# A long convolution with a mixture of experts: four inputs laid in DRAM in the order of their loads

## The chip, the cores and the metric

The kernel runs on one core of a Trainium2 chip. The metric is device microseconds from the start to the end of one execution; less is better. A core has a matrix engine (PE, with its weight loads PEld), VectorE (DVE), ScalarE (ACT), GpSimd (POOL) and SyncE (SP), each with its own stream of instructions, and 16 DMA engines that they share. A DMA is issued by an engine's instruction onto that engine's queue: q1 is SP's, q10 is ACT's, q0 is POOL's. Operands lie in SBUF, in 128 rows (partitions); PE writes to PSUM.

## The reference, cut to what matters

```python
def _attn_ref(x, v, pos_emb, w1, w2):          # x, v: 4 x 11456 x 128, f32
    h_filt = (np.maximum(pos_emb @ w1, 0.0) @ w2) * np.exp(-0.01 * pos)[:, None]
    u = x * v
    L = 2 * S
    Uf = np.fft.rfft(u, n=L, axis=1)
    Hf = np.fft.rfft(h_filt, n=L, axis=0)
    y = np.fft.irfft(Uf * Hf[None, :, :], n=L, axis=1)[:, :S, :]
    return x * y
def _moe_ref(x, w_skip, w_gate, w1, w2):       # 45824 tokens, 8 experts of width 1024
    xc = x[x @ w_skip > 0]
    ...
    y[mask] = gate_w[mask, None] * (np.maximum(xc[mask] @ w1[e], 0.0) @ w2[e])
    out[do_compute] = xc + y
```

The product u of x and v is convolved with a filter that is itself computed from pos_emb, multiplied by x once more, and the tokens with a positive skip score then go through the expert that their gate chooses. This change concerns the convolution and the last multiplication by x.

## The kernel before, in words

The sequence is cut into 3 blocks (NB) of L = 60 x 64 tokens (K1 x N2). A block's transform is done in two stages: matrices over the 60, then, for each of the 60 frequencies, a 128 x 128 matrix over the 64 (with the twiddle factors in it). The 128 channels are split into two halves of 64 (DH), so each stage is passed twice.

**First stage** (class First, L104; `first_phase`, L279). A step handles 8 of the 64 columns of one block and one half of the channels; there are 24 steps to a half (STEPS) and 48 in all. `load` (L143) fetches x and v for a step, 480 KB each, into tiles of 120 rows x 1024 numbers; its DMAs at L150 are on SP's queue. There are three tiles of each (XV), and `ahead` issues a step's load once the tile of three steps before has been multiplied. `mult` (L163) forms u on DVE; in the first pass ACT and DVE split it into a rounded and a remaining part (L169, L170); PE multiplies (L158), ACT copies the sums out of PSUM (L159), and ACT issues one store of 960 KB to x1d in DRAM (L193), in pieces of 1 KB. The filter's own work (`filt`, L197) is dealt out between: its input post, 3 MB in rows of 8 KB on 64 partitions, comes in six loads on ACT's queue (L225); its stores to x1d, 360 KB each in pieces of 768 bytes, are issued by ACT too (L246). The first pass and one step of the second (25 steps) run in this stage.

**Second stage** (`freq_phase`, L306). It goes over 60 pairs of frequencies, 30 to a half. `load` (L332) fetches for each pair its two matrices, c2 (L339, 128 KB), and its data, x1 (L341, 960 KB, rows of 3840 bytes), on SP's queue, three pairs ahead. PE transforms (L372), DVE multiplies by the filter (L366), POOL adds (L368), PE transforms back (L399), ACT copies out (L400), and SP stores to zd (L404). The remaining 23 steps of the first stage's second pass are dealt out among the first 30 pairs.

**Output stage** (`out_phase`, L801). 32 chunks of 3 blocks. `load` (L839) fetches, five blocks ahead, z from zd (L848, 480 KB, pieces of 1 KB) and x once more, ox (L850, 256 KB, 128 rows of 2 KB), on SP's queue. PE does the last transform (L862), DVE multiplies by x (L863), the tokens' scores are taken, and POOL scatters each row to its expert's place in DRAM (L950, 384 indirect DMAs). `START` sets at which step each chunk begins; the first scatter comes in the step of the seventh product. 31 slots of experts' work are dealt out into this stage, and 62 more follow it (`late_slots`).

The host function `arrays` lays out the inputs before the launch, outside the measured time. Before the change `tokens` gives x and v the order (column of 64, row of 60, block, half, batch, channel). One step's load takes from it, for each of its 120 rows, four pieces of 1 KB; rows lie 6 KB apart. c2 lies as (frequency, row, column), and a pair's load takes two pieces of 512 bytes for each row. xo holds a chunk's three blocks side by side, so a block's rows are 2 KB with 6 KB from one to the next.

Of the kernel before, what the change touches and what calls it, by code (L numbers as in the profile page):

```python
# [19 lines left out]
B, S, D = 4, 11456, 128  # L20
E, F = 8, 1024
NB = 3
K1, N2 = 60, 64
L = K1 * N2
H2 = N2 // 2
NS = NB * B
N = L * NS
DH = D // 2
# [23 lines left out]
def tables():  # L52

    k1 = np.arange(K1)
    k2 = np.arange(N2)
    n2 = np.arange(N2)
    n1 = np.arange(K1)
    th = 2 * np.pi * n1[:, None] * (k1[None, :] + 0.25) / K1
    c1 = np.zeros((2, K1, 2, K1, 2))
    c1f = np.zeros((64, 2, 2, K1, 2))  # L60
    for p in range(2):
        c1[p, :, p] = c1f[:K1, p, p] = np.stack([np.cos(th), -np.sin(th)], axis=-1)
    ph = 2 * np.pi * n2[None, :, None] * (k1[:, None, None] + 0.25 + K1 * k2[None, None, :]) / L
    c2 = np.zeros((K1, 128, 128))
    c2[:, :64, :64] = np.cos(ph)
    c2[:, 64:, :64] = np.sin(ph)
    c2[:, :64, 64:] = -np.sin(ph)
    c2[:, 64:, 64:] = np.cos(ph)
    ps = 2 * np.pi * k2[:, None] * n2[None, :] / N2
    c3 = np.zeros((128, 2, 128))  # L70
    c3[:64, 0, :64] = np.cos(ps)
    c3[64:, 0, :64] = -np.sin(ps)
    c3[:64, 0, 64:] = np.sin(ps)
    c3[64:, 0, 64:] = np.cos(ps)
    c3[:64, 1, :64] = -np.sin(ps)
    c3[64:, 1, :64] = -np.cos(ps)
    c3[:64, 1, 64:] = np.cos(ps)
    c3[64:, 1, 64:] = -np.sin(ps)
    c3 = np.ascontiguousarray(c3.reshape(128, 2, 2, 64).transpose(0, 1, 3, 2)).reshape(128, 2, 128)
    al = 2 * np.pi * (k1[:, None, None] + 0.25) * (N2 * n1[None, None, :] + n2[None, :, None]) / L  # L80
    c4 = np.zeros((2 * K1, N2, 64))
    c4[:K1, :, :K1] = np.cos(al) / L
    c4[K1:, :, :K1] = -np.sin(al) / L
    pos = np.arange(S, dtype=np.float32)
    win = np.zeros(NB * L, np.float32)
    win[:S] = np.exp(np.float32(-0.01) * pos)
    winp = np.zeros((2, 64, NB, H2), np.float32)
    winp[:, :60] = win.reshape(NB, 60, 2, H2).transpose(2, 1, 0, 3)
    row = np.arange(128)[:, None] * NS + np.arange(NS)

    e = np.arange(E)
    shift = np.zeros((E, 2, E))
    shift[e, 0, e] = -1
    shift[e[1:], 0, e[:-1]] = 1
    shift[-1, 0, -1] = 0
    shift[:, 1] = e[:, None] <= e[None, :]
    bump = np.where(e < E - 1, CAP, 2 * DUMMY)
    f = np.float32
    winp = winp.transpose(1, 0, 2, 3)
    return {  # L100
        "c1": c1.reshape(2 * K1, 2, 2 * K1).astype(f), "c1f": c1f.reshape(128, 2, 2 * K1).astype(f),
        "c2": c2.astype(f), "c3": c3.astype(f),
        "c4": np.ascontiguousarray(c4.reshape(2 * K1, 2, H2, 64).transpose(0, 2, 1, 3)).astype(f),
        "win": winp.reshape(128, NB * H2), "idb": row.astype(f),  # L104
        "rev": np.tile(np.arange(E, 0, -1, dtype=f), (128, 1)),
        "tri": (np.arange(128)[:, None] < np.arange(128)[None, :]).astype(np.float16),
        "iota": np.tile(np.arange(NTAB, dtype=f), (E, 1)),
        "shift": shift.astype(f), "bump": bump.reshape(E, 1).astype(f),
    }


class First:


    Q = 4
# [25 lines left out]
            self.loaded += 1  # L141

    def load(self, step):  # L143
        nc, Q = self.nc, self.Q
        h, r = divmod(step, self.STEPS)
        blk, ch = divmod(r, N2 // (2 * Q))
        self.tiles[step] = []
        for a, nm in enumerate("xv"):
            t = self.xv[a][step % self.XV]
            nc.sync.dma_start(  # L150
                t.rearrange("n (q c) -> n q c", q=Q),
                self.i[nm][ch * 2 * Q:(ch + 1) * 2 * Q, :, blk, h].rearrange("(q p) n b d -> (p n) q (b d)", p=2))
            self.tiles[step].append(t)

    def first(self, xs, terms, pool):
# [144 lines left out]
def freq_phase(tc, nc, i, fi, zd, c3, loads):  # L300
# [6 lines left out]
    with (  # L307
# [24 lines left out]
        def load(n):  # L332
            h, k = divmod(n, K1 // 2)
            if n == K1 // 2:
                for _ in todo:
                    pass
            ks = slice(2 * k, 2 * k + 2)
            c2 = qx.tile([128, 2, 128], F32, name="c2")
            nc.sync.dma_start(c2, i["c2"][ks].rearrange("k r m -> r k m"))  # L339
            x1 = qx.tile([128, 2, NS + NB, DH], F32, name="x1")  # L340
            nc.sync.dma_start(x1, fi.x1d[h][ks].rearrange("k c n (s d) -> (c n) k s d", d=DH))  # L341
            return x1, c2
# [68 lines left out]
        todo = second()  # L411
        ys = {}
        xs = {n: load(n) for n in range(QX - 1)}
        for _ in range(LEAD):
            next(todo)
        g = {0: filt(*xs[0])}
        for n in range(ALL + LAG):
            back = backer(n - LAG, ys.pop(n - LAG)) if n >= LAG else lambda blk: None
            if n + QX - 1 < ALL:
                xs[n + QX - 1] = load(n + QX - 1)  # L420
            if n > K1 // 2 and n % 2:
                next(loads, None)
            if n < ALL:
                def ahead():
                    if n + 1 < ALL:
                        g[n + 1] = filt(*xs[n + 1])
                x1, c2 = xs.pop(n)
                ys[n] = forward(x1, c2, g.pop(n), back, ahead)
            else:
                for blk in range(NB):  # L430
                    back(blk)
# [369 lines left out]
def out_phase(tc, i, out, zd, xs, ex, consts):  # L801


    nc = tc.nc
    NT = NS
    NCH = H2
    with (
# [3 lines left out]
      with (  # L811
# [20 lines left out]
        chunks = {}  # L832

        BW = B * DH
# [4 lines left out]
        def load(q):  # L839

            ch, blk = divmod(q, NB)
            if q >= NB * NCH:
                return
            if blk == 0 and ch % C4 == 0:
                c4s[ch // C4] = ob.tile([2 * K1, C4, 2, 64], F32, name="c4", bufs=2)
                nc.sync.dma_start(c4s[ch // C4], i["c4"][:, ch:ch + C4])
            z = ob.tile([2 * K1, 4, BW], F32, name="zt", bufs=ZT)
            nc.sync.dma_start(z, zs[ch][:, :, blk * BW:(blk + 1) * BW])  # L848
            x = ob.tile([128, 2, B, DH], F32, name="ox", bufs=ZT)
            nc.sync.dma_start(x, i["xo"][ch][:, blk * 2 * BW:(blk + 1) * 2 * BW])  # L850
            zx[q] = z, x

        def product(ch, blk):
# [113 lines left out]
        for q in range(ZT - 1):  # L967
            load(q)
# [14 lines left out]
        def produced(ch, blk):  # L983
            product(ch, blk)
            load(NB * ch + blk + ZT - 1)
# [3 lines left out]
        steps = {}  # L989
# [9 lines left out]
        for t in sorted(steps):  # L999
            todo = sorted(steps[t], key=lambda v: v[0])  # L1000
            if todo[0][0] != 0:
                todo.insert(0, (0, lambda: None, ()))
            for n, (rank, f, args) in enumerate(todo):
                f(*args)
                if n == 0:
                    next(work, None)
            if tables and next(tables[0], tables) is tables:
                tables.pop(0)
            credit += PACE - 1
            while credit >= 1:  # L1010
                credit -= 1
                next(work, None)
        while tables:
            if next(tables[0], tables) is tables:
                tables.pop(0)
            next(work, None)
# [34 lines left out]
def arrays(inputs):  # L1051
    a = {k: np.ascontiguousarray(v) for k, v in inputs.items()}

    def tokens(v):
        v = np.concatenate([v, np.zeros((B, NB * L - S, D), v.dtype)], axis=1)
        return np.ascontiguousarray(v.reshape(B, NB, K1, N2, 2, DH).transpose(3, 2, 1, 4, 0, 5))
    x = tokens(a["x"])

    def chunks(v):

        v = v.reshape(2, H2, K1, -1).transpose(1, 0, 2, 3)
        return np.concatenate([v, np.zeros((H2, 2, 64 - K1, v.shape[-1]), v.dtype)], axis=2).reshape(H2, 128, -1)
    return {
        "x": x, "v": tokens(a["v"]), "xo": chunks(x),
        "post": np.ascontiguousarray(a["pos_emb"].T), "w1": a["w1"], "w2": a["w2"],
        "wskip": a["moe_w_skip"].reshape(D, 1), "wgate": a["moe_w_gate"],
        "moe_w1": a["moe_w1"], "moe_w2": a["moe_w2"], **tables(),
    }
# [19 lines left out]
```

## Time and profile before

| what | value |
|---|---|
| median of 3 runs | 1788.04 us (1786.23 to 1788.09) |
| profiled execution | 1784.53 us |
| its span, first to last instruction | 1782.8 us |
| granted TensorE clock, mean | 0.962 |
| busy: PE, DVE, ACT, POOL | 1609.6, 1211.6, 890.1, 1099.3 us |
| DMA records on q1, q10, q0 | 220600, 64007, 18240 |
| x and v loads (L150) | 96 of 480 KB |
| c2 loads (L339) | 60 of 128 KB |
| ox loads (L850) | 96 of 256 KB |

How to read the lines of the prediction. A row of stretches gives start and end in us, the length, then for each engine the busy us and the number of instructions, the granted share of the TensorE clock, the mean busy share of the 16 DMA engines and the GB/s that they moved. A queue's line gives the number of DMA records (one contiguous piece each, and a few of 4 bytes that signal the end), the MB, and the time of its records as a share of 16 engines over the stretch; the share can pass 1, since records overlap a little. A line of waits names who waited, for whom, how long in all, how often, and the longest. A line of an instruction group gives durations in ns as minimum/median/maximum.

### The profile page before, as it was taken

The page shows a single profiled execution, that of the slowest core. Times are in us where ns is not written, and L with a number is a line of the kernel's source. Part 1 is how long each engine was busy: PE and PEld are TensorE (multiplying, and loading weights), DVE is VectorE, ACT ScalarE, POOL GpSimd, SP SyncE. Part 2 cuts the span into 40 slices and gives each one's busy share as a digit, 9 for nine tenths or more (in the row PEclk, how much of TensorE's full clock was granted, in tenths as well). Part 3 has the DMA queues.
Part 4 walks back from the last instruction along what each step waited for, and adds up shares of the span by engine and source line. Part 5 has one row for each costly group of instructions (what it writes and reads, how often), then busy time and mean ns, then how long its engine had stood idle before and what let it go on. Part 6 is the DMA issues. An engine that isn't in the chain of part 4 may idle for free. (4 is left out here: it accounts for less than half of the span.)

```text
span 1782.8 us, 29560 instructions
## 1 busy us (share of the span) xinstructions
PE 1609.6 (90%) x9450; PEld 1155.1 (65%) x9450; DVE 1211.6 (68%) x2134; ACT 890.1 (50%) x1512; POOL 1099.3 (62%) x816
## 2 busy tenths in 40 slices
PE   3988869999999999996759999999986999999997
PEld 2555545555556666553226766666665999999997
DVE  2434258777778999994446654554542799989996
ACT  2655435545454444442214554444443677777774
POOL 0000048667678999995377777777777366655665
PEclk8999889999999999998979999999998999999999
DMA  9999899999998899875999998999932222222221
GB/s 236 355 304 303 269 278 280 320 320 320 326 286 240 259 284 283 269 206 141 255 281 256 266 261 230 233 235 243 242 104 72 68 63 66 64 65 65 64 66 45
DMA packets 303004, 379.82 MB, mean 213 GB/s; under 512 B 24524, under 2 KB 238916, under 8 KB 302527
## 3 DMA queue, kind: packets, MB, share of 16 engines
q1 hardware_dynamic: 220600, 291.42, 57.4%
q10 hardware_dynamic: 64007, 62.57, 11.5%
q0 software_dynamic: 18240, 23.92, 4.8%
q8 instruction: 76, 1.25, 0.3%
q14 instruction: 81, 0.66, 0.1%
HBM read 216.88 MB, written 174.99 MB: 220 GB/s over the span
## 5 line engine op out<-in xcount | busy, mean ns | idle before, releaser
L950 POOL DMA_INDIRECT xs<-xm,to x384 | 390.1, 1016 | 162.5 <-issue 100.5
L399 PE MATMUL zps<-y,c 128*128 128x512 f32 x720 | 338.5, 594 | 0.0
L368 POOL TENSOR_TENSOR y<-y,p 128x1024 f32<-128x1024 f32 x120 | 282.8, 2357 | 89.2 <-DVE y L366 84.5
L610 POOL DMA_INDIRECT out<-o,ids x124 | 168.8, 1361 | 137.5 <-DVE o L617 116.4
L366 DVE TENSOR_TENSOR p<-xp,g 128x1024 f32<-128x1024 f32 x180 | 218.0, 1211 | 44.7 <-PE xp L372 29.2
L366 DVE TENSOR_TENSOR y<-xp,gc 128x1024 f32<-128x1024 f32 x180 | 218.2, 1212 | 21.9 <-PE xp L372 21.9
L582 DVE TENSOR_TENSOR ws<-wf,ws 128x1024 fp32r<-128x1024 f32 x155 | 189.2, 1220 | 43.7 <-ACT ws L577 36.2
L355 POOL TENSOR_TENSOR g<-gc 128x256 f32<-128x256 f32 x60 | 50.3, 839 | 258.2 <-ACT gc L353 258.2
L372 PEld LDWEIGHTS xp<-x,c 128*128 128x128 f32 x720 | 137.3, 191 | 99.6 <-issue 78.3
L400 ACT COPY z<-zps 128x512 f32<-128x512 f32 x180 | 103.9, 586 | 191.8 <-PE zps L399 190.3
L399 PEld LDWEIGHTS zps<-y,c 128*128 128x128 f32 x720 | 134.4, 190 | 98.8 <-issue 89.0
L372 PE MATMUL xp<-x,c 128*128 128x256 f32 x720 | 186.9, 382 | 4.7 <-DVE p L366 4.7
L353 ACT COPY gc<-t 64x384 f32<-64x384 f32 x240 | 113.5, 473 | 120.2 <-DVE y L366 71.7
L577 ACT CAST ws<-wf 128x1024 fp32r x155 | 161.6, 1043 | 17.7 <-issue 11.5
L159 ACT COPY wf<-ps 120x512 f32<-120x512 f32 x192 | 110.3, 589 | 89.3 <-PE ps L158 43.5
L604 PE MATMUL hp<-hl,ws 128*128 128x256 f32 x496 | 151.1, 305 | 1.0 <-DVE hh L724 1.0
L724 DVE SCALAR_TENSOR_TENSOR hh<-hp,hh 128x1024 fp32r<-128x1024 f32 x124 | 150.6, 1215 | 0.8 <-ACT hh L723 0.8
L368 POOL TENSOR_TENSOR p<-p,p 128x1024 f32<-128x1024 f32 x60 | 149.5, 2492 | 0.0
L863 DVE TENSOR_TENSOR xm<-y,ox 128x512 f32<-128x512 f32 x96 | 66.2, 689 | 120.4 <-PE y L862 56.7
L158 PE MATMUL ps<-ur,c1r 120*120 120x512 f32 x300 | 103.9, 479 | 41.0 <-ACT ur L169 27.9
L606 PE MATMUL hp<-hl,ws 128*128 128x256 f32 x496 | 140.9, 284 | 0.0
L605 PE MATMUL hp<-hl,ws 128*128 128x256 f32 x496 | 140.6, 284 | 0.0
(149 smaller groups left out, 3483.4 us busy)
## 6 DMA issues: line engine op xcount, KB each, us to landing
x<-x1d SPq DMA_DIRECT2D x60, 960.0 KB
x1d<-wf ACTq DMA_DIRECT2D x48, 960.0 KB
zd<-z SPq DMA_DIRECT2D x120, 384.0 KB
zt<-zd SPq DMA_DIRECT2D x96, 480.0 KB
out<-xm SPq DMA_DIRECT2D x96, 260.0 KB
ox<-xo SPq DMA_DIRECT2D x96, 256.0 KB
wf<-x SPq DMA_DIRECT2D x48, 480.0 KB
wf<-v SPq DMA_DIRECT2D x48, 480.0 KB
```

Source lines behind the costliest of these rows:

```text
L366: nc.vector.tensor_tensor(o, x[:, None].broadcast_to([128, 2, B, D]), v[:, :, None, :].broadcast_to([128, 2, B, D]), ALU.mult)
L368: add = lambda o, v: nc.gpsimd.tensor_tensor(o, o, v, ALU.add)
L372: nc.tensor.matmul(x[:, :, k], c2[:, k], x1[:, k, blk * B:(blk + 1) * B, :], start=True, stop=True)
L399: nc.tensor.matmul(zps, c3[:, a, :], y[:, blk, a], start=(a == 0), stop=(a == 1))
L577: nc.scalar.copy(w[:, 0], (self.w1f, self.w2f)[which][:, ds(self.where(nc.scalar, tb), F)])
L582: eng.tensor_tensor(w[:, 1], src[:, ds(self.where(eng, tb), F)], w[:, 0].bitcast(F32), ALU.subtract)
L604: nc.tensor.matmul(hp, w[:, 0, c], hl[:, 0], start=True, stop=False)
L605: nc.tensor.matmul(hp, w[:, 0, c], hl[:, 1], start=False, stop=False)
L606: nc.tensor.matmul(hp, w[:, 1, c], hl[:, 0], start=False, stop=True)
L610: ins = nc.gpsimd.indirect_dma_start(out=self.rows, out_offset=bass.IndirectOffsetOnAxis(ap=ids[:, j:j + 1], axis=0), in_=o, in_offset=Non ...
L724: nc.vector.scalar_tensor_tensor(h[:, 1], hp, 0.0, h[:, 0].bitcast(F32), ALU.max, ALU.subtract)
L950: ex.row_write(nc.gpsimd.indirect_dma_start(out=xs, out_offset=bass.IndirectOffsetOnAxis(ap=to[:, t:t + 1], axis=0), in_=xm[:, part * B + ...
```

## The change

x and v are laid out on the host as (step, 120 rows, 1024 numbers), so that a step's load is one stretch of DRAM with 4 KB to each row of the tile. c2 is laid out by pairs, with both matrices' parts of a row side by side: one stretch, 1 KB to a row. xo is laid out by chunk and block: one stretch, 2 KB to a row. The tiles, the numbers in them, the queue, the order of all instructions and the other loads are as before.

```diff
-        "c2": c2.astype(f), "c3": c3.astype(f),
+        "c2": np.ascontiguousarray(c2.reshape(K1 // 2, 2, 128, 128).transpose(0, 2, 1, 3)).astype(f), "c3": c3.astype(f),
...
     def load(self, step):
-        nc, Q = self.nc, self.Q
-        h, r = divmod(step, self.STEPS)
-        blk, ch = divmod(r, N2 // (2 * Q))
+        nc = self.nc
         self.tiles[step] = []
         for a, nm in enumerate("xv"):
             t = self.xv[a][step % self.XV]
-            nc.sync.dma_start(
-                t.rearrange("n (q c) -> n q c", q=Q),
-                self.i[nm][ch * 2 * Q:(ch + 1) * 2 * Q, :, blk, h].rearrange("(q p) n b d -> (p n) q (b d)", p=2))
+            nc.sync.dma_start(t, self.i[nm][step])
...
             c2 = qx.tile([128, 2, 128], F32, name="c2")
-            nc.sync.dma_start(c2, i["c2"][ks].rearrange("k r m -> r k m"))
+            nc.sync.dma_start(c2, i["c2"][k])
...
-            nc.sync.dma_start(x, i["xo"][ch][:, blk * 2 * BW:(blk + 1) * 2 * BW])
+            nc.sync.dma_start(x, i["xo"][ch, blk])
...
-    def tokens(v):
-        v = np.concatenate([v, np.zeros((B, NB * L - S, D), v.dtype)], axis=1)
-        return np.ascontiguousarray(v.reshape(B, NB, K1, N2, 2, DH).transpose(3, 2, 1, 4, 0, 5))
-    x = tokens(a["x"])
+    def padded(v):
+        return np.concatenate([v, np.zeros((B, NB * L - S, D), v.dtype)], axis=1)
+
+    def steps(v):
+
+        Q = First.Q
+        v = padded(v).reshape(B, NB, K1, N2 // (2 * Q), Q, 2, 2, DH).transpose(6, 1, 3, 5, 2, 4, 0, 7)
+        return np.ascontiguousarray(v.reshape(2 * First.STEPS, 2 * K1, Q * B * DH))
 
     def chunks(v):
 
-        v = v.reshape(2, H2, K1, -1).transpose(1, 0, 2, 3)
-        return np.concatenate([v, np.zeros((H2, 2, 64 - K1, v.shape[-1]), v.dtype)], axis=2).reshape(H2, 128, -1)
+        v = padded(v).reshape(B, NB, K1, 2, H2, 2, DH).transpose(4, 1, 3, 2, 5, 0, 6)
+        v = np.concatenate([v, np.zeros((H2, NB, 2, 64 - K1, *v.shape[4:]), v.dtype)], axis=3)
+        return v.reshape(H2, NB, 128, 2 * B * DH)
     return {
-        "x": x, "v": tokens(a["v"]), "xo": chunks(x),
+        "x": steps(a["x"]), "v": steps(a["v"]), "xo": chunks(a["x"]),
```

## The prediction

> **What bounds the kernel now.** The chain of work that ended last breaks off after three pieces here, so I read the profile by stages: first the page's DMA lines, then busy time by stretch, then the DMA records of short stretches in which one kind of transfer runs alone.
>
> ```profile
> span 1782.8 us, 29560 instructions
> DMA  9999899999998899875999998999932222222221
> q1 hardware_dynamic: 220600, 291.42, 57.4%
> q10 hardware_dynamic: 64007, 62.57, 11.5%
> ...
> x1d<-wf ACTq DMA_DIRECT2D x48, 960.0 KB
> ...
> wf<-x SPq DMA_DIRECT2D x48, 480.0 KB
> wf<-v SPq DMA_DIRECT2D x48, 480.0 KB
> ```
>
> A step of the first stage loads 2 x 480 KB and stores 960 KB. q1 is SP's queue, on which all changed loads are issued; q10 is ACT's. The transfer engines look full over the first three quarters, but that alone doesn't make them the bound. The stretches (columns: length, busy PE, PEld, DVE, ACT, POOL, granted clock, DMA share, GB/s) say where they are:
>
> ```profile
> 0.00:40.00 40.00, 11.17 (x30) 7.69 (x31) 9.56 (x11) 9.86 (x15) 0.20 (x4) 0.92 0.98 222
> 40.00:100.00 60.00, 56.47 (x268) 36.29 (x267) 25.87 (x25) 41.91 (x69) 0.00 (x0) 0.97 1.02 351
> 100.00:205.00 105.00, 83.65 (x412) 52.37 (x411) 40.25 (x41) 51.95 (x90) 0.00 (x0) 0.91 0.96 302
> 260.00:520.00 260.00, 260.00 (x798) 146.88 (x797) 204.14 (x182) 129.59 (x240) 187.50 (x93) 1.00 1.00 308
> 560.00:800.00 240.00, 240.00 (x795) 146.63 (x794) 238.91 (x207) 101.29 (x198) 220.58 (x114) 1.00 0.87 260
> 840.00:880.00 40.00, 27.40 (x185) 10.77 (x185) 15.54 (x52) 8.91 (x22) 5.70 (x6) 0.88 1.04 247
> 880.00:1320.00 440.00, 393.17 (x3096) 268.86 (x3095) 237.39 (x922) 200.39 (x391) 338.26 (x335) 0.95 0.91 241
> 1400.00:1760.00 360.00, 360.00 (x3027) 360.00 (x3026) 325.72 (x524) 260.89 (x350) 217.56 (x174) 1.00 0.24 65
> ```
>
> From 260 to 520 PE is busy all 260 us, from 560 to 800 both PE (240 of 240) and DVE (238.91) are, and from 1400 on PE again with the DMA at 0.24. Faster transfers are worth nothing there. Between 880 and 1320 POOL issues its row scatters one behind the other:
>
> ```profile
> POOL xs L950 <- issue: 100.5, 330, 0.3
> POOL xs L950 <- DMA zt<-zd: 45.9, 1, 45.9
> ```
>
> 335 scatters in 440 us are one per 1.31 us, and 330 of the 384 waited for nothing but their issue; a single one, the first, waited for a transfer. So that stage has only its start (840 to 880) to give. What remains is the first stage, up to about 205 us: no engine is full, and the DMA share is 0.96 to 1.02. ACT shows how it binds: it issues the stores, and is held while it does:
>
> ```profile
> L246 ACTq DMA_DIRECT2D x1d<-fx x32: 322/1190/3087, 81.9 to 222.6; - x32
> ACT wf L159 <- DMA x1d<-wf: 16.5, 2, 8.5
> ACT wf L159 <- DMA x1d<-fx: 9.0, 1, 9.0
> SPq L150 <- DMA wf<-v: 25.0, 5, 20.0
> ```
>
> An unhindered issue is 322 ns, the median one 1190 and the longest 3087.
>
> **What a record costs.** Two stretches give two equations (queue line: records, MB, share of 16 engines). From 50 to 56 us loads and stores of 1 KB run side by side, from 238 to 241 SP's x1 loads run with rows of 3840 B and matrix rows of 512 B:
>
> ```profile
> q10 hardware_dynamic: 1083, 1.09, 51.3%
> q1 hardware_dynamic: 1085, 1.08, 50.7%
> ...
> DMA packets 579, 1.21 MB, mean 402 GB/s; under 512 B 33, under 2 KB 312, under 8 KB 579
> q1 hardware_dynamic: 579, 1.21, 104.4%
> ```
>
> 0.507 x 16 x 6 us = 48.7 us for 1085 records and 1.08 MB; 1.044 x 16 x 3 = 50.1 us for 579 and 1.21 MB. The solution is 6.9 ns per record and 38.1 ns per 1000 B. That makes 45.9 ns for 1 KB, 163 for 4 KB, 26 for 512 B, 85 for 2 KB. 4096 B in four records cost 184 ns, in one 163.
>
> [...]
>
> **The change, part by part.**
>
> *x and v (96 loads, L150).* Each load goes from 480 records of 1 KB to 120 of 4 KB: 480 x 45.9 = 22.0 us of engine time against 19.6, so 2.5 us less. 48 of the loads fall to the second pass, which runs beside a full PE (260 to 520): worth 0 while PE is full; without that cover 48 x 2.5 / 16 = 7.5 us. How many count in the first stage? From 40 to 205 us:
>
> ```profile
> DMA packets 55414, 52.84 MB, mean 320 GB/s; under 512 B 1345, under 2 KB 55405, under 8 KB 55405
> q1 hardware_dynamic: 22726, 22.57, 40.4%
> ```
>
> 22.57 MB are 46 loads of 0.49 MB. 46 x 2.5 / 16 = **7.1 us**, if the share stays near 1. What is late next is PE: 83.65 of 105 us, 56.47 of 60; so the gain is at risk between 40 and 100, not after.
>
> *The first 40 us.* Loads alone are far slower than loads beside stores. From 32 to 37 us only x and v run; from 18 to 28 us they share the engines with the filter's 8 KB post rows on q10:
>
> ```profile
> DMA packets 1270, 1.26 MB, mean 253 GB/s; under 512 B 37, under 2 KB 1270, under 8 KB 1270
> q1 hardware_dynamic: 1270, 1.26, 104.7%
> ...
> DMA packets 560, 2.21 MB, mean 221 GB/s; under 512 B 52, under 2 KB 324, under 8 KB 328
> q10 hardware_dynamic: 288, 1.93, 86.2%
> q1 hardware_dynamic: 272, 0.28, 14.3%
> ...
> q1 hardware_dynamic: 4950, 4.92, 53.1%
> ```
>
> 1.047 x 80 us / 1270 are 66 ns per 1 KB instead of 45.9. In the first 40 us (the last line) q1 moves 4.92 MB, ten loads. Either strided reading causes the slow rate, and then they win 10 x (480 x 66 - 120 x 163) / 16 = 8 us; or it is the tile's 120 rows, and nothing changes. The x1 loads above, contiguous, with 128 rows, reach 402 GB/s; the post rows, 8 KB in one stretch but only 64 rows, 221. Length alone doesn't lift the rate, so I take the second. Ends: 0 and -8. The fence shows one thing more: 288 records of 8 KB against 272 of 1 KB. The two queues take turns by record, whatever the size. With 4 KB a turn the loads of step 2 come in earlier, and SP's 20.0 us wait for a v load shortens, while the posts, and ACT behind them, get later. I put 1 us of gain on it.
>
> [...]
>
> *c2 (60 loads, L339).* 256 records of 512 B become 128 of 1 KB: 60 x (256 x 26 - 128 x 45.9) / 16 = 3 us of engine time, nearly all beside a full PE or DVE; without that cover, 3 us. Only the loads ahead of the stage's first product, at 228 to 237 us, are bare: 0.1 us. I take 0.
>
> *ox (96 loads, L850).* 128 records of 2 KB before and after; only the step between rows goes from 6 KB to 2 KB. From 842 to 862 us:
>
> ```profile
> DMA packets 4030, 4.75 MB, mean 237 GB/s; under 512 B 190, under 2 KB 3247, under 8 KB 4029
> q1 hardware_dynamic: 4029, 4.73, 104.2%
> ```
>
> 1.042 x 320 us for 4.73 MB are 70 ns per 1000 B, 145 for 2 KB instead of 85. Were the pitch the cause, the seven loads ahead of the first scatter would win 7 x 128 x 60 / 16 = 3.4 us. The zt rows of the same stretch stay strided, so I take 0. Ends: 0 and -3.4. No instruction is added or moved on any engine, no wait is added, and SP's order stays.
>
> *Sum*: -7.1 - 1 = **-8 us**. The profiled execution took 1784.53 us (span 1782.8 plus 1.7 around it): 1776.5. The median of the runs shown, 1788.04, lies 3.5 above the profiled execution; so for a median I predict **1780**.
>
> **The rivals.**
>
> *A, slower: the loads crowd out the stores.* Taking turns by record, a 1 KB store waits behind a 4 KB load: for a step's 240 load records only 240 of its 960 store records go beside them, and 720 follow alone. What stores alone do, from 258 to 262 us with 1 KB rows and from 216 to 218 us with 768 B rows:
>
> ```profile
> DMA packets 983, 0.99 MB, mean 248 GB/s; under 512 B 15, under 2 KB 983, under 8 KB 983
> q10 hardware_dynamic: 835, 0.85, 79.5%
> ...
> DMA packets 845, 0.63 MB, mean 315 GB/s; under 512 B 25, under 2 KB 845, under 8 KB 845
> ```
>
> A step then costs 240 x (163 + 46) / 16 = 3.1 us, plus 0.737 MB at 248 GB/s = 3.0 us: 6.1, against 1.97 MB at 351 GB/s = 5.6 now. 23 steps x 0.5 = +11.5: **1799**. It decides from 295 GB/s for stores alone (3.1 + 0.737/0.295 = 5.6), which lies between the two rows. For it: ACT, which issues the stores, is the held engine. Against: from 100 to 205 us reads and writes are already unmixed (302 GB/s), and there the loads' gain stands.
>
> [...]
>
> *B, hidden:* the first stage is held by PE and ACT with their hand-overs, since PE has 56.47 of 60 us. The transfers get shorter and the steps don't: **1788**. Against: PE falls to 83.65 of 105 after that, with the DMA at 0.96.
>
> *C, more:* strided reading is what slows reads alone. -7.1 - 8 - 3.4 = -18.5: **1769.5**. Against: the post rows.
>
> *D, the change doesn't do it:* records stay 1 KB. Then q1 keeps its 220600 records and the time is B's. I hold it within B.
>
> **How the numbers follow.** Forecast 0.46, A 0.22, B with D 0.20, C 0.12. 0.2%, about what a measurement of this kernel can tell from no change, is 3.6 us. Faster: 0.42 of the forecast and C: 0.54. Same: 0.04 of the forecast, B, 0.02 of A: 0.26. Slower: 0.20 from A. The forecast's own range is 1776 (4 us more from the first 40 us, where I took 1 between 0 and 8) to 1785 (half of the 7.1 lost to PE between 40 and 100). The range over all cases leaves out the outer part of A (above 1796): 1769 to 1796.
>
> **What would show it.** The stores of the first pass, first and last start at the row's end:
>
> ```profile
> L193 ACTq DMA_DIRECT2D x1d<-wf x25: 323/324/1702, 34.5 to 226.0; - x25
> ```
>
> q1 must fall by 96 x 360 + 60 x 128 = 42240 records, to about 178400. The first pass's last store must be issued 8 us before 226.0, and everything behind it keep its length: 260 us of full PE, the scatters' 1.31 us. For A, the issue at L246 would rise above 1190 ns in the median, and GB/s between 40 and 100 fall below 351. For C, the first 40 us would carry far more than 222 GB/s and the first scatter come earlier against the stage's start. I am wrong above all if stores alone run at the lower of the two rows.

## The result, and the profile after

The changed kernel is slower, 1796.52 us in the median of 5 runs against 1786.42 us before: a ratio of 1.006 (95% interval 1.0043 to 1.0077), about 10 us. The ratios leave out slow executions (beside the first experiments below, the kernel before took 2774.97 us once, at a granted clock of 0.657, with a median of 1786.5), so that they need not equal the ratio of the medians beside them. The forecast of 1780 us was wrong in its sign, and rival A, with 1799 us, was the nearest. The profiled execution of the changed kernel took 1796.25 us, its span 11.7 us more than before. Two things on the text above: in the kernel before, First begins at L112, `first_phase` at L266, `filt` at L198 and `freq_phase` at L300; in the kernel after, code behind the shorter `load` stands four lines higher, so that L193 is L189 and L159 is L155.

The page of the changed kernel, first the span, then the shares of the DMA engines over 40 slices, then SP's queue:

```profile
span 1794.5 us, 29560 instructions
...
DMA  9999988999998899874999988988842222222221
...
q1 hardware_dynamic: 178360, 291.42, 56.2%
```

The records fell by 42240, as they had to (rival D is out), and the bytes are the same. The stretches of the changed kernel, in the columns of before:

```profile
0.00:40.00 40.00, 12.94 (x39) 9.16 (x40) 9.57 (x11) 10.35 (x15) 0.20 (x4) 1.00 0.90 202
40.00:100.00 60.00, 46.62 (x205) 28.70 (x204) 22.05 (x21) 34.46 (x59) 0.00 (x0) 0.90 0.98 325
100.00:205.00 105.00, 88.41 (x455) 56.02 (x455) 41.10 (x41) 56.58 (x96) 0.00 (x0) 0.93 0.95 305
260.00:520.00 260.00, 254.59 (x776) 143.63 (x775) 200.40 (x178) 125.76 (x233) 184.48 (x92) 1.00 0.96 299
```

Two places have changed. Between 40 and 100 us the DMA engines move 325 GB/s instead of 351, and PE is busy 46.62 us instead of 56.47. Between 260 and 520 us PE, which had been busy all the time, lacks 5.4 us, in two gaps of 2.3 and 3.1. Where the 11.7 us arise can be read from the starts of the 48 stores of the first stage. These are the rows of that store's issue, all 48 of them, before and then after; behind the second stands the row of the first 25 (the first pass and one step) in the changed kernel:

```profile
L193 ACTq DMA_DIRECT2D x1d<-wf x48: 323/324/1702, 34.5 to 539.9; - x48
```

```profile
L189 ACTq DMA_DIRECT2D x1d<-wf x48: 323/323/2055, 33.0 to 552.4; - x48
...
L189 ACTq DMA_DIRECT2D x1d<-wf x25: 323/324/2055, 33.0 to 232.6; - x25
```

The 25th store is 6.6 us late (232.6 for 226.0), the 48th 12.5 us (552.4 for 539.9). So some 6.6 us are lost in the first stage and 5.9 in the second; behind that the two kernels run alike to within 0.8 us.

Within the first stage the loss sits at one spot. In the waits of the first 60 us ACT waits for post loads, and in the changed kernel then for a store that it had issued itself. Before and after:

```profile
ACT ur L169 <- DMA post<-post: 14.8, 1, 14.8
```

```profile
ACT ur L165 <- DMA post<-post: 18.0, 1, 18.0
ACT wf L155 <- DMA x1d<-wf: 11.4, 1, 11.4
```

Before, the second wait did not occur in this stretch. It is, seen in the order of time, ACT alone (start, duration, and in brackets the idle time before it and what ended that):

```profile
42.15 0.32 ACTq L189 DMA_DIRECT2D x1d<-wf  x1
...
54.53 0.58 ACT L155 COPY wf<-ps 120x512 f32<-120x512 f32 x1 [11.41 <-DMA x1d<-wf]
```

Three output tiles (XS) hold the stage's results until they are stored. The fourth step's first copy needs the first step's tile, and the store of that tile, issued at 32.97 us, lands only now. What the two queues did meanwhile, from 44 to 50 us, before and then after:

```profile
q1 hardware_dynamic: 1240, 1.24, 61.3%
q10 hardware_dynamic: 848, 0.85, 41.0%
```

```profile
DMA packets 754, 1.75 MB, mean 291 GB/s; under 512 B 45, under 2 KB 422, under 8 KB 754
...
q1 hardware_dynamic: 377, 1.36, 75.4%
q10 hardware_dynamic: 377, 0.39, 22.5%
```

377 records on the one queue (332 of 4 KB and 45 that signal an end), 377 on the other: they take turns, and since a load's record is now 4 KB and a store's 1 KB, the stores get 0.39 MB in 6 us, where they had 0.85. Equal counts could also come of turns of several records each; the times of the records in the trace exclude that. In 371 of the 377 stores a record of the other queue begins 3 or 4 ns before the store's end; one of the stores' own queue does so in 30, no more than at other moments. A turn is one record. That is rival A's mechanism. But the total fell too, from 349 to 291 GB/s, and this is not for stores alone being slow. From 54 to 58 us, with the waiting loads done, the stores had the engines almost to themselves (8 of 1417 records are loads):

```profile
DMA packets 1417, 1.46 MB, mean 365 GB/s; under 512 B 15, under 2 KB 1409, under 8 KB 1417
...
q10 hardware_dynamic: 1409, 1.43, 100.4%
```

They moved 365 GB/s. Loads alone did not gain; here they are from 12 to 14 us:

```profile
DMA packets 140, 0.51 MB, mean 257 GB/s; under 512 B 15, under 2 KB 15, under 8 KB 140
...
q1 hardware_dynamic: 136, 0.51, 90.5%
```

257 GB/s against 253 with strided 1 KB records: the compact reading of longer records did not speed up loads alone. Rival C is out for x and v.

Last, the ordinary steps. Issues of stores 5 and 9 of the stage, before and after:

```profile
56.43 0.34 ACTq L193 DMA_DIRECT2D x1d<-wf  x1
...
80.30 0.32 ACTq L193 DMA_DIRECT2D x1d<-wf  x1
```

```profile
64.03 0.32 ACTq L189 DMA_DIRECT2D x1d<-wf  x1
...
87.92 0.32 ACTq L189 DMA_DIRECT2D x1d<-wf  x1
```

Four steps take 23.87 us before and 23.89 us after. The stretches between these issues show why, before and after:

```profile
56.43:80.30 23.87, 23.87 (x130) 15.90 (x129) 11.76 (x12) 17.35 (x29) 0.00 (x0) 1.00 1.02 357
```

```profile
64.03:87.92 23.89, 23.89 (x130) 15.90 (x129) 11.76 (x12) 17.39 (x29) 0.00 (x0) 1.00 0.98 339
```

PE is busy all the time, with the same 130 matmuls. These steps are as long as PE's work, and the transfers are hidden behind it. From store 9 to store 25 PE has gaps; there the two traces take 145.7 and 144.7 us, and a kernel with 1 KB records in one stretch (below) 146.8, so that one trace cannot tell a gain of 1 us from none.

### The profile page after: what moved, and what is told of

Its sections match the earlier page's. It is cut to its first block, busy times and chain, and to the rows that moved or that the text cites. A ratio compares the mean times of both kernels' runs of the same rounds, so it can differ in the third digit from the quotient of the medians.

```text
span 1794.5 us, 29560 instructions
## 1 busy us (share of the span) xinstructions
PE 1614.5 (90%) x9450; PEld 1155.4 (64%) x9450; DVE 1214.8 (68%) x2134; ACT 889.1 (50%) x1512; POOL 1097.5 (61%) x816
## 3 DMA queue, kind: packets, MB, share of 16 engines
q1 hardware_dynamic: 178360, 291.42, 56.2%
q10 hardware_dynamic: 64007, 62.57, 11.7%
## 5 line engine op out<-in xcount | busy, mean ns | idle before, releaser
L578 DVE TENSOR_TENSOR ws<-wf,ws 128x1024 fp32r<-128x1024 f32 x155 | 189.2, 1220 | 45.2 <-ACT ws L573 36.0
L155 ACT COPY wf<-ps 120x512 f32<-120x512 f32 x192 | 110.2, 590 | 91.8 <-PE ps L154 43.4
L600 PE MATMUL hp<-hl,ws 128*128 128x256 f32 x496 | 151.5, 305 | 0.7 <-DVE hh L720 0.7
L666 PEld LDWEIGHTS bank<-wd,h 128*128 128x128 f32 x992 | 121.1, 200 | 31.5 <-issue 31.4
L602 PE MATMUL hp<-hl,ws 128*128 128x256 f32 x496 | 141.3, 285 | 0.0
```

What stands on the lines that cost most here:

```text
L578: eng.tensor_tensor(w[:, 1], src[:, ds(self.where(eng, tb), F)], w[:, 0].bitcast(F32), ALU.subtract)
L600: nc.tensor.matmul(hp, w[:, 0, c], hl[:, 0], start=True, stop=False)
L602: nc.tensor.matmul(hp, w[:, 1, c], hl[:, 0], start=False, stop=True)
L666: nc.tensor.matmul(bank[:, j * D:(j + 1) * D], h[f // 2][:, f % 2, j * 128:(j + 1) * 128], wd[s][:, f * D:(f + 1) * D], start=(f == 0), st ...
```

## The experiments

The diffs show the changed load, against the kernel after; the host's matching order of the data is left out. The theory after the result (T): the queues take turns by record, so long load records push back the stores and post loads of ACT's queue where several loads wait. Rivals: the addresses (R: a load out of one stretch slows things), the other two inputs (C, here meaning c2 and ox), a loss in every step (P, against a loss that is all from the start, S), and L, that the turns cost only because loads into 120 rows cannot run faster than some 250 GB/s (alone they moved 253 before and 257 after).

All of them, each against runs of the kernel before on the same chip:

| experiment | median us | before us | ratio, 95% interval | store 4 at us | store 25 at us |
|---|---|---|---|---|---|
| before (the profile shown) | | | | 50.53 | 226.0 |
| after (the profile shown) | 1796.52 | 1786.42 | 1.006, 1.0043 to 1.0077 | 58.04 | 232.6 |
| x and v only | 1797.29 | 1786.5 | 1.005, 1.0034 to 1.0066 | 55.27 | 238.9 |
| c2 and ox only | 1787.95 | 1786.5 | 1.0002, 0.9985 to 1.0019 | 50.76 | 228.5 |
| one stretch, 1 KB | 1786.32 | 1786.5 | 0.9994, 0.998 to 1.0007 | 50.32 | 226.9 |
| strided, 4 KB | 1796.54 | 1786.5 | 1.0047, 1.0031 to 1.0063 | 56.56 | 233.9 |
| one stretch, 2 KB | 2012.86 | 2007.75 | 1.0028, 0.9997 to 1.006 | 51.64 | 229.4 |
| 1 KB for 8 steps, then 4 KB | 2011.76 | 2007.75 | 1.0053, 1.0015 to 1.0091 | 50.03 | 231.5 |
| 4 KB for 8 steps, then 1 KB | 2016.54 | 2007.75 | 1.0037, 1.0001 to 1.0073 | 57.44 | 235.0 |
| 128 rows, 1 KB (first run) | 2004.24 | 2007.75 | 1.0003, 0.9972 to 1.0035 | 45.2 | 221.8 |
| 128 rows, 4 KB | 1785.14 | 1785.98 | 0.999, 0.9977 to 1.0003 | 48.21 | 226.7 |
| 128 rows, 1 KB (second run) | 1780.99 | 1785.98 | 0.9969, 0.9954 to 0.9983 | 44.72 | 222.6 |
| 128 rows, 1 KB, post in 128 rows | 1772.95 | 1785.98 | 0.9934, 0.9916 to 0.9951 | 38.19 | 213.9 |
| 4 KB, 120 rows, post in 128 rows | 1792.68 | 1785.98 | 1.0031, 1.0019 to 1.0044 | 47.34 | 230.1 |

The four with some 2010 us ran on another chip, whose granted clock was lower (0.91 on the mean of a run, 0.96 elsewhere). Their first two stages run at the pace of the other traces; the later ones don't, and their intervals are wide. They are used by their traces of the first two stages.

**Which of the inputs.** x and v as in the kernel after, the other two as before:

```diff
-            nc.sync.dma_start(c2, i["c2"][k])
+            nc.sync.dma_start(c2, i["c2"][ks].rearrange("k r m -> r k m"))
...
-            nc.sync.dma_start(x, i["xo"][ch, blk])
+            nc.sync.dma_start(x, i["xo"][ch][:, blk * 2 * BW:(blk + 1) * 2 * BW])
```

> x and v as in the changed kernel, c2 and ox as before. Theory T (turns): the two queues take turns by record, so a 4 KB load record on SP's queue pushes back the post loads and the stores on ACT's queue wherever loads are waiting (the first 58 us, and stalls in the second stage); c2 and ox have no part. T expects the whole loss: +9 to +11 us against the kernel before, the store of step 3 issued near 58 us as in the changed kernel (50.5 before). Rival C (c2 or ox cause part of it): +6 us or less.

And the reverse, c2 and ox as after, x and v as before:

```diff
-            nc.sync.dma_start(t, self.i[nm][step])
+            nc.sync.dma_start(
+                t.rearrange("n (q c) -> n q c", q=Q),
+                self.i[nm][ch * 2 * Q:(ch + 1) * 2 * Q, :, blk, h].rearrange("(q p) n b d -> (p n) q (b d)", p=2))
```

> c2 and ox as in the changed kernel, x and v as before: the other half. T expects no change within 2 us. Rival C: +4 us or more.

x and v alone give 1.005, c2 and ox alone 1.0002. The loss belongs to x and v, though the fourth store, at 55.27 us, is not quite as late as the 58 expected. In the waits of the first 60 us with x and v alone the stall stands again:

```profile
ACT wf L155 <- DMA x1d<-wf: 10.2, 1, 10.2
```

With c2 and ox alone it is absent. C is out for these two as well.

**Record or address.** One stretch, but with the pieces in such an order that a record is 1 KB:

```diff
-            nc.sync.dma_start(t, self.i[nm][step])
+            nc.sync.dma_start(t.rearrange("n (q c) -> n q c", q=Q), self.i[nm][step].rearrange("q n c -> n q c"))
```

> The changed kernel, but a load of x or v lies as one stretch of 480 KB with its pieces ordered so that each record is 1 KB again (480 records to a load). T expects the time of the kernel before, within 3 us, and the store of step 3 near 50 us. Rival R (addresses: reading one compact stretch is what slows the loads or the stores beside them): the changed kernel's time, +10 us.

And 4 KB records whose rows lie 24 KB apart:

```diff
-            nc.sync.dma_start(t, self.i[nm][step])
+            nc.sync.dma_start(t, self.i[nm][ch][:, blk, h])
```

> The changed kernel, but the 4 KB rows of a load of x or v lie 24 KB apart, as far apart in proportion as in the kernel before; 120 records of 4 KB to a load. T expects the changed kernel's time, +8 to +12 us. Rival R: the time of the kernel before.

Four loads that differ in two things, and the time follows one of them: 0.9994 with 1 KB records out of one stretch, 1.0047 with 4 KB records from afar. Where the bytes lay didn't count in these four, the record's length did. The stretches from 40 to 100 and from 260 to 520 us, first of the one-stretch 1 KB kernel, then of the strided 4 KB one:

```profile
40.00:100.00 60.00, 55.91 (x260) 35.59 (x260) 24.93 (x24) 41.56 (x69) 0.00 (x0) 0.95 1.02 355
...
260.00:520.00 260.00, 259.52 (x796) 146.38 (x795) 205.20 (x182) 128.93 (x238) 187.35 (x93) 1.00 0.99 308
```

```profile
40.00:100.00 60.00, 48.04 (x221) 30.05 (x219) 21.52 (x22) 35.17 (x59) 0.00 (x0) 0.89 0.98 328
...
260.00:520.00 260.00, 257.53 (x788) 144.93 (x788) 204.39 (x181) 127.66 (x238) 187.79 (x94) 1.00 0.97 305
```

Both signs of the changed kernel, PE's gap at the start and the missing us in the second stage (2.5 here, 5.4 there), come with the 4 KB and go with the 1 KB. Of the 2.5, 0.6 lie before 270 us, where the stage begins later than before because the first stage ended later. R is out. Loads alone followed neither length nor address by much: 253 GB/s before and 257 after, as above. Of the one-stretch 1 KB kernel, from 32 to 35 us:

```profile
DMA packets 682, 0.68 MB, mean 226 GB/s; under 512 B 21, under 2 KB 682, under 8 KB 682
```

The strided 4 KB kernel had 266 GB/s from 12 to 14 us.

**How long a record, and when.** 2 KB records:

```diff
-            nc.sync.dma_start(t, self.i[nm][step])
+            nc.sync.dma_start(t.rearrange("n (q c) -> n q c", q=2), self.i[nm][step].rearrange("q n c -> n q c"))
```

> The changed kernel with x and v in records of 2 KB (240 to a load), still one stretch. Turns by record (T) expect the loss to grow with the record: between 1 KB (0) and 4 KB (+9), +2 to +6 us; the store of step 3 between 50.5 and 57 us. A rival in which only the number of records counts (fewer is better or all the same) expects 0 or less.

ACT's stall at the start is there, and shorter:

```profile
ACT wf L155 <- DMA x1d<-wf: 3.1, 1, 3.1
```

0, 3.1 and 11.4 us for 1, 2 and 4 KB in one stretch. The time itself, 1.0028 with an interval that includes 1, is as expected but doesn't decide. Then the two lengths in one kernel, first 1 KB for steps 0 to 7 and 4 KB for the rest, then the reverse (`step >= 8` in the same line):

```diff
-            nc.sync.dma_start(t, self.i[nm][step])
+            s = self.i[nm][step]
+            if step < 8:
+                nc.sync.dma_start(t.rearrange("n (q c) -> n q c", q=Q), s.rearrange("(q n c) -> n q c", q=Q, n=2 * K1))
+            else:
+                nc.sync.dma_start(t, s.rearrange("(n c) -> n c", n=2 * K1))
```

> The changed kernel, but the loads of the first 8 steps have 1 KB records (one stretch each), the other 40 steps 4 KB. T with the loss at the start and in the second stage: the start's part (about 7 us) is gone, the store of step 3 near 50.5 us; +2 to +5 us are left, from the second stage. Rival S (the loss is all from the start): 0. Rival P (a loss in every step, as rival A of the prediction has it): +8 us.

> The other half: 4 KB records for the first 8 steps, 1 KB for the other 40. T: +5 to +8 us, the store of step 3 at 55 to 58 us, no loss behind it. Rival S: +9 to +11. Rival P: +2.

With 4 KB for the first eight steps, the fourth store came at 57.44 us and the 25th at 235.0, 9 us late; behind that the second pass took as long as before. This is as expected. The reverse was only half right. The fourth store was on time, but the loss came later: when the 4 KB loads set in, ACT waited for a store (the stretch from 55 to 80 us), and the 25th store was 5.5 us late, not on time.

```profile
ACT wf L159 <- DMA x1d<-wf: 3.9, 1, 3.9
```

So the loss doesn't belong to the first microseconds; S is out. In these two traces it appears where the long records begin, over a few steps, and the steps after it keep their pace, which speaks against P. The times don't decide it: 1.0053 with an interval from 1.0015 to 1.0091 lies above the 2 to 5 us that T expected for the first of the two, and nearer to P's 8; the reverse, 1.0037 (1.0001 to 1.0073), is near the 5 to 8 that T expected. The last experiment below has a trace in which later steps lose time too.

**Are the turns enough to explain it?** The changed kernel with loads into 128 rows, the last 8 of them zeros that nobody reads:

```diff
-        self.xv = [[piece(1) for _ in range(self.XV)] for _ in "xv"]
+        self.xv = [[piece(1, 128) for _ in range(self.XV)] for _ in "xv"]
...
-            self.tiles[step].append(t)
+            self.tiles[step].append(t[0:2 * K1])
```

> The changed kernel (4 KB records, one stretch) with 128 instead of 120 rows to a load of x or v (8 rows of zeros that nobody reads). In the changed kernel loads and stores, taking turns by record, moved only 291 GB/s from 44 to 50 us. T (the turns alone cost: a store record gets one turn for 4 KB of loads): the loss stays, +4 to +9 us, and step 3's store is issued at 52 us or later. Rival L (the turns cost only because loads of 120 rows cannot run faster than some 250 GB/s, so that the engine time which the stores lose is not made good): with 128 rows the loads run at 350 GB/s or more, both are done as early as before, and the loss is gone: -4 to +1 us, step 3's store at 45 to 49 us.

The same with 1 KB records, in two runs. The first, on the chip with the lower clock, left the comparison open (1.0003, 0.9972 to 1.0035):

> 1 KB records out of one stretch, but each load fills 128 rows of its tile instead of 120 (8 rows of zeros that nobody reads, 6.7% more bytes). If the slow rate of loads alone (253 GB/s) comes from the 120 rows, loads alone run at 300 GB/s or more and the kernel is 2 to 6 us faster than before; the turns stay even. If it comes from the strided reading or from DRAM, the rate stays near 250 and the time is that of the kernel before or up to 2 us more.

> 1 KB records out of one stretch, 128 rows to a load: the same kernel as in the run on a chip whose later stages ran 200 us slower, where its own trace had step 3's store at 45.2 us and the end of the first stage 4 us earlier than in the kernel before, and where the comparison stayed open. Expected now: -2 to -6 us.

With 128 rows and 4 KB the loss is gone against the kernel before (0.999, interval up to 1.0003), and the fourth store comes at 48.21 us, as L expected and T alone did not. From 36 to 42 us the queues still take turns, 482 loads and 50 end signals to 486 stores, but now they move 412 GB/s where the 120-row loads had 291:

```profile
DMA packets 1018, 2.47 MB, mean 412 GB/s; under 512 B 50, under 2 KB 536, under 8 KB 1018
...
q1 hardware_dynamic: 532, 1.97, 80.3%
q10 hardware_dynamic: 486, 0.50, 23.3%
```

The second stage is whole again:

```profile
260.00:520.00 260.00, 260.00 (x798) 146.82 (x797) 204.15 (x182) 129.72 (x240) 187.44 (x94) 1.00 0.94 313
```

Yet the turns still cost something. ACT waits 7.6 us for its store in the first 60 us, and the kernel with 128 rows and 1 KB, on the same chip, takes 1780.99 us against 1785.14. Long records cost 4 us with 128 rows and 10 with 120. So two causes act together: the turns handed the engines to the loads (75.4% of their time from 44 to 50 us), and the loads into 120 rows couldn't use what they were handed (291 GB/s in all, where 128 rows had 412).

That 120 rows hold the rate is seen from loads alone, here 128 rows and 1 KB in the second run, from 28 to 32 us:

```profile
DMA packets 1392, 1.39 MB, mean 347 GB/s; under 512 B 35, under 2 KB 1392, under 8 KB 1392
```

347 GB/s, where the same 1 KB records out of one stretch gave 226 in 120 rows, and strided ones 253. Though 6.7% more bytes are moved, that kernel is faster than the one before: 0.9969. The count of records shows one difference besides the rows. q1 has 179224 with 128 rows and 4 KB against 178360 in the changed kernel, 864 more: 8 rows for each of the 96 loads, and one more end signal for each, 16 instead of 15. Whether one of the 16 engines stays out of a load into 120 rows is not shown; it would be a sixteenth, where a quarter to a third is missing (253 and 226 GB/s for 347).

**The post loads too.** Each of the three blocks of post laid as 128 rows of 8 KB, once with 128-row 1 KB loads, once with the loads of the changed kernel:

```diff
-            for a in range(2):
-                rows = slice(a * 64, a * 64 + 64)
-                at = blk * L + a * HALF
-                have = min(HALF, S - at)
-                if have < HALF:
-                    nc.vector.memset(pt[rows, have:], 0.0)
-                nc.scalar.dma_start(pt[rows, :have], i["post"][:, at:at + have])
+            nc.scalar.dma_start(pt, i["post"][blk])
```

> 128 rows, 1 KB records, and the post input laid so that each of its three blocks is one load of 128 rows by 8 KB instead of two of 64 rows. If 64 rows are what holds the post loads at some 215 GB/s, they end 6 to 8 us earlier and the first stage gets another 3 to 6 us shorter: -6 to -11 us in all. If long rows or DRAM hold them, the rate stays near 220 and the time is that of the kernel with 128 rows alone.

> The changed kernel (120 rows, 4 KB records) with the post input in loads of 128 rows. The part of the loss that comes from the post loads being pushed back (ACT's first cast at 24.9 instead of 20.4 us) goes: cast at 18 to 21 us. If the stall behind the first store (11.4 us) stays, the kernel is +3 to +8 us slower than the kernel before; if the post loads were all of it, 0 or less.

In the first of them the post loads, from 14 to 20 us:

```profile
DMA packets 599, 2.49 MB, mean 416 GB/s; under 512 B 32, under 2 KB 332, under 8 KB 332
...
q10 hardware_dynamic: 299, 2.19, 87.0%
q1 hardware_dynamic: 300, 0.31, 14.5%
```

416 GB/s instead of 221, and again turns by record, 299 to 300: in 266 of the 267 post records a load's record begins 3 or 4 ns before their end. The post rows make this difference, not those of the loads, since 128-row loads beside posts of 64 rows gave 223 (the second 128-row 1 KB run, from 18 to 26 us):

```profile
DMA packets 483, 1.79 MB, mean 223 GB/s; under 512 B 49, under 2 KB 290, under 8 KB 322
```

The 25th store comes at 213.9 us and the kernel takes 1772.95 us, 0.9934 (0.9916 to 0.9951): 13.0 us less than the kernel before on the same chip, more than the 6 to 11 expected, and 23.6 less than the 1796.52 us of the changed kernel, which come from another series of runs. With the long records and 120 rows kept, the post loads in 128 rows bring ACT's first cast to 15.2 us (24.9 in the changed kernel, 20.4 before), but 1.0031 remains. That is not as expected: a loss should have remained only with the stall, and the stall is nearly gone.

```profile
ACT wf L155 <- DMA x1d<-wf: 2.7, 1, 2.7
```

The fourth store comes 3.2 us earlier than before, and still the 25th comes 4.1 us later: from store 9 to store 25 this trace takes 152.7 us, the kernel before 145.7. Here later steps lose time, and what holds them is not shown. The second stage lacks its us as in the changed kernel:

```profile
260.00:520.00 260.00, 255.45 (x775) 143.45 (x774) 199.64 (x177) 125.64 (x234) 184.39 (x91) 0.99 0.96 298
```

## Why the prediction was wrong

The forecast was -7.1 us for the steps of the first stage, -1 for the first 40 us and 0 for the second pass. The traces have -0.9 us from the fourth store to the 25th, +7.5 up to the fourth, +5.9 from the 25th to the 48th and -0.8 behind it: 11.7 in all. The gain was missing, and the sign came from the other two terms, which put nothing on what longer load records do to ACT's queue.

- *x and v, -7.1 us.* The term failed twice. It was "7.1 us, if the share stays near 1", and a cheaper record shortens a step only where the DMA engines set its length. I took an engine share of 0.96 to 1.02 for the bound, but in the four steps shown PE is busy all the time: 23.87 and 23.89 us. Stores 5 and 9 of the 128-row 1 KB kernel, whose loads are a third faster when alone, say the same:

```profile
50.62 0.32 ACTq L189 DMA_DIRECT2D x1d<-wf  x1
...
74.49 0.32 ACTq L189 DMA_DIRECT2D x1d<-wf  x1
```

  23.87 us once more. Rival B was right for these steps, by PE's work rather than by its hand-overs with ACT. And the saving of 11% in engine time did not appear. Of the changed kernel, from 40 to 205 us:

```profile
q1 hardware_dynamic: 6088, 22.15, 40.0%
```

  0.400 x 16 x 165 us for 22.15 MB are 47.7 us per MB; the row of the kernel before (22.57 MB at 40.4%) gives 47.3. A 4 KB record was priced at 163 ns; in the 6 us of turns above, 0.754 x 96 us for 377 records are 192 ns each, the end signals counted. With 128 rows the stretch from 40 to 205 us has 22.70 MB at 37.7%, 43.8 us per MB: there 7% are saved.
- *The first 40 us, -1 us.* The turns by record, 288 against 272, were read rightly, and that "the posts, and ACT behind them, get later" was said, but nothing was put on it. The post loads and ACT's stores, on the queue that holds the stage up, came later: the first wait grew from 14.8 to 18.0 us, and a new one of 11.4 us appeared. The net was a loss of 7.5 us at the fourth store (58.04 for 50.53).
- *The second pass, "worth 0 while PE is full".* A full PE didn't cover a late store. ACT copies what PE makes, and between 260 and 520 us it waits 4.5 us for a store of x1d:

```profile
PE ps L154 <- ACT wf L155: 5.4, 2, 3.1
...
ACT z L396 <- DMA x1d<-wf: 4.5, 1, 4.5
```

  PE waits for ACT twice, 5.4 us in all. The first gap, 2.3 us, comes at the end of ACT's wait for the store. Before the second, 3.1 us, ACT stood idle too; what held it there is not shown. With 128 rows and 4 KB PE has its 260 us again.
- *Rival A.* Its mechanism, the loads crowding out the stores, is shown, its 1799 us lay 2.5 us off, and both its signs came: 325 GB/s between 40 and 100 us, and a median of 1350 ns for the filter's store issues at L246 (L242 after), which had 1190. Its working was not right: it priced stores alone at 248 GB/s, in every step. That row was not of stores alone, since 148 of its 983 records are q1's; the stores of the changed kernel moved 365 from 54 to 58 us, all but alone. The loss of the changed kernel comes in two places and not in each step, and part of its cause is the slow 120-row load. The condition "295 GB/s for stores alone" decided nothing. That the sum came out near was chance.
- *The 120 rows.* "Or it is the tile's 120 rows, and nothing changes": right for loads alone, 257 GB/s after. I didn't carry it on to the mixture, where the loads' limit became everyone's when they held most of the engines' time (75.4% against 22.5%). The post loads show an effect of the rows too, 221 GB/s with 64 of them and 416 with 128. Why 120 rows ran at 253 where 128 rows ran at 347 is not shown.
- *Turns.* The prediction read turns by record from the counts alone, 288 to 272. That was not enough: turns of equally many records each would give equal counts too. The records' times, 371 of 377 and 266 of 267, say that here a turn is one record.
- *c2 and ox.* 0 predicted, 1.0002 measured (0.9985 to 1.0019).

## What to carry to other kernels

Before a transfer's records are made longer, look at what shares the DMA engines with it: here two queues took turns by record (after 371 of 377 stores a record of the other queue), so the one with the longer records moved more of the bytes (1.36 against 0.39 MB in 6 us), and if the other one carries what an engine waits for, the kernel can get slower, as here (1.006), though each transfer has fewer records. A DMA share near 1 is not yet a bound (it was 1.02 over four steps in which PE was busy all 23.87 us); take a few steps in the middle of a stage and see whether another engine is busy in all of them. The rows of a tile can be worth more than the length of its records: 128 instead of 120 rows took loads alone from 226 to 347 GB/s, and 128 instead of 64 took the post loads, with the loads beside them, from 223 to 416.

## What the runs showed of the hardware

Two queues alternated record by record, 1 KB stores with 4 KB loads and 8 KB posts with 1 KB loads: of 377 stores, 371 were followed by a record of the other queue, and of 267 posts, 266. Loads into 120 rows moved 207 to 266 GB/s alone, whether a record had 1 or 4 KB and whether it was read from one stretch or in strides (207 with c2 and ox only, from 32 to 37 us; 226, 253, 257 and 266 as above). Beside 1 KB stores in equal turns the limit didn't show with 1 KB loads (1083 to 1085 records and 2.17 MB in 6 us, 362 GB/s); beside 4 KB loads it did (291 GB/s from 44 to 50 us). Loads of 1 KB into 128 rows moved 347 GB/s from 28 to 32 us. A load into 120 rows signalled its end with 15 records, one into 128 rows with 16 (864 more records on q1: 8 rows and one signal for each of 96 loads). Stores of 120 rows with 1 KB records moved 365 GB/s almost alone.
